# Loading two tiles of x from GpSimd's queue, dividing the fillers around their transposes, and storing one more late tile in halves

## The chip, the cores and the metric

The kernel runs on one core of a Trainium2 chip. The metric is the device time of one execution in microseconds. The kernel before has a median of 232.59 us over 3 runs.

## The reference

x is 16 x 512 x 1024 in bf16, that is 8192 tokens of 1024 values; w is 1024 x 1024 in bf16; b has 1024 values. In every column of w, each group of four successive rows keeps the two values of largest magnitude and sets the others to zero. The result is x times that pruned w, plus b.

```
wg = w.reshape(G, M, D)                     # M = 4
mag = jnp.abs(wg)
order = jnp.argsort(mag, 1)
thr = jnp.take_along_axis(mag, order[:, M - N:M - N + 1, :], 1)   # N = 2
mask = mag >= thr
wp = (wg * mask).reshape(D, D)
return jnp.einsum("bsd,df->bsf", x, wp) + b
```

## The kernel before, in words

The 8192 tokens are 64 tiles of 128. A tile's result is 128 x 1024: two PSUM banks of 512 columns, each the sum of eight matmuls over 128 values of the inner dimension.

TensorE cannot wait until all of w is pruned, so the work starts with seven tiles (0 to 6) that take the pruned w piece by piece. w is loaded in pieces (`load_w`, line 100); VectorE computes magnitude, threshold, mask and product of each (`Piece.do`, line 164; steps `abs`, `hi`, `lo`, `t1`, `t2`, `thr`, `mask`, `mult`). The first piece, columns 0 to 255 of the upper half of w, comes in two loads of 128 KB: one on SyncE's queue (lines 118 and 98), called w0a here, one on ScalarE's queue (line 119), called w0b. The seven tiles of x are loaded as they lie (`load_x`, line 103): tiles 5 and 6 on ScalarE's queue, tiles 3 and 4, tile 2, and tiles 0 and 1 on SyncE's. The loads are called x3, x5, x2 and x0 here, after their first tile. TensorE transposes them (`transpose`, line 188: four 128 x 128 transposes a tile, recorded at line 193; each needs the identity that GpSimd makes first), ScalarE copies the result to SBUF (`copy_xt`, line 196), and `mm_piece` (line 213) multiplies, recorded at line 229.

The order on each engine is written out by hand: `order` (line 266) lists tokens for TensorE, VectorE, ScalarE and SyncE, and the helper `seq` keeps each engine's instructions in that order. T3a is the transposes of tile 3, C3a its copy, M3.0yp a part of the multiplication of tile 3 with piece 0 (which follows the VectorE step mult0yp), W0.0 the spreading of pruned pieces into the natural layout `wp_nat` by DMA, E and A the first matmuls from that layout. A token F with a number is that many fillers; `order` has none before the change.

Ahead of the first transpose TensorE runs fillers (line 138): matmuls on constants whose result nobody reads. There are six of 512 columns and then fourteen of 128 columns (lines 404 and 405).

After the start, tiles 7 to 11 and the lower halves of tiles 0 to 6 use x that a DMA has transposed (`load_lead`, `load_low`), and tiles 12 to 63 come in batches by DMA transpose (`load_nat`). Each tile's result is evicted by VectorE with the bias (`evac`, line 435) and stored from ScalarE's queue (`store`, line 445). The last `LATE` tiles are stored in halves of 128 KB, the others whole, 256 KB.

Of the kernel before, what the change touches and what calls it, by code (L numbers as in the profile page):

```python
# [11 lines left out]
def kernel(  # L12
# [7 lines left out]
    nc = tc.nc  # L20
# [22 lines left out]
    STG = 8  # L43
    SOLO = 6
    GROUPS = ((0, 3), (3, 6), (6, 7))
    LATE = 6
    sizes = (4, 8, 8, 8, 8, 8, 8)
    batches = []
    t0 = NPK + LEAD
# [17 lines left out]
    def seq(eng, inst):  # L67
        if eng in tails:
            tc.add_manual_dep(inst.ins, tails[eng].ins.name, NOSYNC, reason="program order")
        tails[eng] = inst  # L70
        return inst

    def pe(i):
        return seq("pe", i)
# [4 lines left out]
    def act(i):  # L79
        return seq("act", i)  # L80
# [13 lines left out]
    bias_sb = const.tile([P, Dout], bf16)  # L94

    def issue(eng, out_, in_):
        q = nc.sync if eng == "sp" else nc.scalar
        return seq(eng, q.dma_start(out_, in_))

    def load_w(g, c0, c1, ma=0, mb=4, eng="sp"):  # L100
        issue(eng, w_sb[:, g, ma:mb, c0:c1], wv[:, g, ma:mb, c0:c1])

    def load_x(ta, tb, eng="sp"):
        xs = const.tile([P, tb - ta, HK], bf16, name=f"x_{ta}")
        issue(eng, xs[:], xf[ta * P:tb * P, :HK].rearrange("(t p) k -> p t k", p=P))
        for t in range(ta, tb):
            x_sb[t] = xs[:, t - ta, :]
# [7 lines left out]

    xnat, held = {}, {}

    load_w(0, 0, 256, 0, 2)
    load_w(0, 0, 256, 2, 4, "act")
    load_x(5, 7, "act")  # L120
    act(nc.scalar.activation(spark[:], nc.const_aps.tensor(1.0, [P, 1], bf16), Act.Abs))
    load_x(3, 5)
    load_x(2, 3)
    load_w(0, 256, 512)
    load_x(0, 2)
# [10 lines left out]
    def filler(n, rep=1):  # L136
        for _ in range(n):
            pe(nc.tensor.matmul(warm_ps[:, :rep * P], lhsT=nc.const_aps.tensor(1.0, [P, P], bf16),  # L138
                                rhs=nc.const_aps.tensor(1.0, [P, rep * P], bf16), start=True, stop=True))
# [4 lines left out]
    def spread(g, c0, c1, ks=range(4), eng="sp"):  # L144
        for k in ks:
            issue(eng, wp_nat[:, 4 * g + k, c0:c1], wp[32 * k:32 * k + 32, g, :, c0:c1])
# [112 lines left out]
    def stage(key):  # L259
        solo = key[1] == "h"  # L260
        q, h, at = (pair_of[key[0]], key[2], int(key[0] != SOLO)) if solo else (key[0], key[1] // 2, key[1] % 2)
        if (q, h) not in staged:
# [2 lines left out]

    order = {
# [124 lines left out]
    def run(queues):  # L391
        while any(queues.values()):
            moved = False
            for eng, toks in queues.items():
                while toks and all(n in written for n in needs(eng, toks[0])):
                    emit(eng, toks[0])
                    tok = toks.pop(0)
                    written.add(tok)
                    if tok[0] == "M" or tok[0].islower():
                        written.update(atoms(tok))  # L400
                    moved = True
            assert moved, queues

    filler(6, 4)
    filler(14)
    run({eng: order[eng].split() for eng in order})

    def load_nat(ta, tb):
# [26 lines left out]
    def evac(o, ps, c0, c1, add=None):  # L435
        if add is None:
            dve(nc.vector.tensor_tensor(o[:, c0:c1], ps, bias_sb[:, c0:c1], op=Alu.add))  # L437
        else:
            dve(nc.vector.tensor_tensor(o[:, c0:c1].rearrange("p (n c) -> p n c", n=2),  # L439
                                        ps.rearrange("p (n c) -> p n c", n=2), add, op=Alu.add))  # L440
# [4 lines left out]
    def store(eng, t, o, c0=0, c1=Dout):  # L445
        issue(eng, rows(t)[:, c0:c1], o[:, c0:c1])
# [25 lines left out]
    for bi, (tb, nb) in enumerate(batches):  # L472
        if bi:
            load_batch(bi + 1)
        for j in range(nb):
# [9 lines left out]
            else:  # L485
# [4 lines left out]
                for h in range(2):  # L490
                    evac(o, pss[h][:], h * FH, (h + 1) * FH)
                    if t >= NT - LATE:
                        store("act", t, o, h * FH, (h + 1) * FH)
                if t < NT - LATE:
                    store("act", t, o)
# [30 lines left out]
```

## Time and profile before

| what | value |
| --- | --- |
| median of 3 runs | 232.59 us (232.45 to 233.13) |
| the profiled execution's own time | 232.89 us |
| its span, first to last instruction | 231.1 us |
| TensorE matmul busy | 226.6 us, 98% of the span |
| VectorE busy | 107.9 us, 47% |
| ScalarE, GpSimd busy | 14.0 us, 17.6 us |

Times in the rows are microseconds from the start of the span. A row of the timeline gives the start, the time that the group took, the engine, the line, the operation, what it writes and reads, the shape and the count. PEld is TensorE's weight load. A row of a table by stage gives the stage's length, each engine's busy time with its count, the granted clock, the share of the DMA engines and the rate.

### The profile page before, as it was taken

How to read it: one execution, taken by the hardware profiler on the slowest of the kernel's cores; microseconds unless marked ns; L12 is line 12 of the kernel's file. 1: busy time of each engine (PE TensorE's matmuls, PEld its weight loads, DVE VectorE, ACT ScalarE, POOL GpSimd, SP SyncE). 2: the span in 40 equal slices, each digit the busy share in tenths (PEclk: the TensorE clock that was granted, in tenths of full speed). 3: DMA queues.
4: the chain of work that ended last, by engine and by line, in shares of the span. 5: the costliest groups of instructions: out<-in, count | busy, mean ns of one | idle time of the engine just before them, and what ended most of it. 6: DMA issues, size and time to landing. Idle time of an engine off the chain costs nothing.

```text
span 231.1 us, 2851 instructions
## 1 busy us (share of the span) xinstructions
PE 226.6 (98%) x1142; PEld 110.9 (48%) x1162; DVE 107.9 (47%) x200; ACT 14.0 (6%) x27; POOL 17.6 (8%) x15
## 2 busy tenths in 40 slices
PE   8999999999999999999999999999999999999995
PEld 5986444444444444444444444444444444444443
DVE  3999877844424424424424424423423423433434
ACT  2874100000000000000000000000000000000000
POOL 1000199700000000000000000000000000000000
PEclk9999999999999999999999999999999999999999
DMA  6999999997399422991259821693128932122122
GB/s 203 276 197 280 164 217 223 297 320 252 124 206 232 155 91 72 237 281 64 75 116 252 222 94 71 162 298 134 65 91 198 273 122 83 54 91 91 53 86 91
DMA packets 79308, 38.19 MB, mean 165 GB/s; under 512 B 64192, under 2 KB 71744, under 8 KB 79296
## 3 DMA queue, kind: packets, MB, share of 16 engines
q1 hardware_dynamic: 68384, 20.75, 43.6%
q10 hardware_dynamic: 10912, 17.27, 20.9%
q8 instruction: 9, 0.15, 0.3%
q14 instruction: 3, 0.02, 0.0%
HBM read 3.28 MB, written 16.78 MB: 87 GB/s over the span
## 4 chain that ended last, share of the span: by engine, by line
PE 98%; issue 0%; DVE 0%
PE ps L242 88%; PE ps L229 5%; PE tp L242 2%; PE ps L138 2%; PE tp L193 1%; PE ps L193 0%; DVE o L437 0%
## 5 line engine op out<-in xcount | busy, mean ns | idle before, releaser
L242 PE MATMUL ps<-wp_nat,xb 128*128 128x512 bf16 (+1 forms) x831 | 178.9, 375 | 0.9
L242 PEld LDWEIGHTS <-xb 128*128 128x128 bf16 x848 | 82.2, 98 | 97.7
L437 DVE TENSOR_TENSOR o<-ps,bias_sb 128x512 bf16<-128x512 f32 (+1 forms) x112 | 71.6, 677 | 113.7 <-PE ps L242 111.4
L433 POOL TENSOR_TENSOR st<-st,bias_sb 128x1024 f32<-128x1024 f32 x8 | 16.7, 2142 | 0.0
L242 PE MATMUL ps<-wp_nat,xlead 128*128 128x512 bf16 x63 | 14.7, 379 | 0.1
L242 PEld LDWEIGHTS <-xlead 128*128 128x128 bf16 x88 | 8.6, 98 | 10.2
L229 PE MATMUL ps<-wp,xt 128*128 128x256 bf16 (+1 forms) x130 | 12.8, 258 | 0.0
L439 DVE TENSOR_TENSOR o<-ps,st 128x512 bf16<-128x512 f32 x16 | 11.1, 691 | 2.8 <-PE ps L242 2.2
L229 PEld LDWEIGHTS <-xt 128*128 128x128 bf16 x130 | 10.9, 98 | 1.1
L242 PE MATMUL ps<-wp_nat,xlow 128*128 128x512 bf16 x47 | 10.6, 379 | 0.1
L264 ACT COPY st<-ps 128x512 f32<-128x512 f32 x14 | 7.4, 600 | 3.2 <-PE ps L229 3.1
L242 PEld LDWEIGHTS <-xlow 128*128 128x128 bf16 x48 | 4.7, 98 | 5.7
L159 DVE TENSOR_TENSOR mag<-mag,hi 128x256 bf16<-128x256 bf16 (+2 forms) x15 | 6.1, 435 | 0.1
L159 DVE TENSOR_TENSOR wp<-w_sb,mag 128x256 bf16<-128x256 bf16 (+2 forms) x15 | 6.1, 435 | 0.1
L242 PE MATMUL tp<-wp_nat,xlead 128*128 128x512 bf16 x23 | 5.8, 380 | 0.0
L138 PE MATMUL ps<-const-bfloat16-1.0 128*128 128x128 bf16 (+1 forms) x20 | 4.2, 408 | 0.8 <-PEq L510 0.8
L169 DVE TENSOR_SCALAR mag<-w_sb 128x512 uint16<-128x512 uint16 (+2 forms) x5 | 2.3, 473 | 3.5 <-DMA w_sb<-in_w_dram 3.5
L138 PEld LDWEIGHTS <-const-bfloat16-1.0 128*128 128x128 bf16 x20 | 2.3, 146 | 2.4 <-issue 2.4
L159 DVE TENSOR_TENSOR hi<-mag 128x512 bf16<-128x512 bf16 (+2 forms) x7 | 3.2, 458 | 0.1
L159 DVE TENSOR_TENSOR lo<-mag 128x512 bf16<-128x512 bf16 (+1 forms) x6 | 3.1, 509 | 0.0
L193 PEld LDWEIGHTS <-x 128*128 128x128 bf16 x28 | 2.3, 124 | 0.3 <-DMA x<-in_x_dram 0.2
L422 POOL COPY pruned<-wp 128x1 bf16<-128x1 bf16 x1 | 0.2, 187 | 26.7 <-DVE wp L159 26.7
(18 smaller groups left out, 18.8 us busy)
## 6 DMA issues: line engine op xcount, KB each, us to landing
out_dram<-o ACTq DMA_DIRECT2D x58, 256.0 KB, 2.4
wp_nat<-wp SPq DMA_DIRECT2D x14, 128.0 KB, 3.2
out_dram<-o ACTq DMA_DIRECT2D x10, 128.0 KB, 1.7
w_sb<-in_w_dram SPq DMA_DIRECT2D x2, 512.0 KB, 5.5
w_sb<-in_w_dram SPq DMA_DIRECT2D x3, 256.0 KB, 5.1
x<-in_x_dram SPq DMA_DIRECT2D x2, 256.0 KB, 4.3
x<-in_x_dram ACTq DMA_DIRECT2D x1, 256.0 KB, 4.0
bias_sb<-in_b_dram SPq DMA_DIRECT2D x1, 256.0 KB, 4.7
```

The lines of the kernel that those rows point to most:

```text
L138: pe(nc.tensor.matmul(warm_ps[:, :rep * P], lhsT=nc.const_aps.tensor(1.0, [P, P], bf16), rhs=nc.const_aps.tensor(1.0, [P, rep * P], bf16), ...
L159: dve(nc.vector.tensor_tensor(out, a, b_, op=op))
L169: dve(nc.vector.tensor_single_scalar(mag.bitcast(u16), w_.bitcast(u16), 0x7FFF, op=Alu.bitwise_and))
L193: pe(nc.tensor.transpose(tp[:, m, :], xg[:, m, :], ident[:]))
L229: pe(nc.tensor.matmul(ps[:, c0 + d:c1 + d], lhsT=xpk[t][:, m, :], rhs=wp[:, g, m, c0:c1], start=(new and m == ms.start), stop=(left[key] = ...
L242: pe(nc.tensor.matmul(ps, lhsT=xt[:, kt - koff, :], rhs=wp_nat[:, kt, c0:c1], start=(kt == first), stop=(kt == last)))
L264: act(nc.scalar.copy(staged[(q, h)][:, at, :, :].rearrange("p t c -> p (t c)"), ps_open.pop(key)[:]))
L422: pool(nc.gpsimd.tensor_copy(out=pruned[:], in_=wp[:, 1, 3, Dout - 1:]))
L433: pool(nc.gpsimd.tensor_tensor(st[:], st[:], bias.to_broadcast([P, 2, 2, CW]), op=Alu.add))
L437: dve(nc.vector.tensor_tensor(o[:, c0:c1], ps, bias_sb[:, c0:c1], op=Alu.add))
L439: dve(nc.vector.tensor_tensor(o[:, c0:c1].rearrange("p (n c) -> p n c", n=2), ps.rearrange("p (n c) -> p n c", n=2), add, op=Alu.add))
```

## The change

Tiles 3 and 4 of x are no longer loaded from SyncE's queue, in its second place, but from GpSimd's, ahead of the identity. Of the fourteen narrow fillers four stay ahead of the transposes of tiles 3 and 4; six more stand behind these, ahead of the transposes of tiles 5 and 6; four are gone. `LATE` goes from 6 to 7, so tile 57 is stored in two halves.

```diff
-    LATE = 6
+    LATE = 7
...
     def issue(eng, out_, in_):
-        q = nc.sync if eng == "sp" else nc.scalar
+        q = {"sp": nc.sync, "act": nc.scalar, "pool": nc.gpsimd}[eng]
         return seq(eng, q.dma_start(out_, in_))
...
+    load_x(3, 5, "pool")
     load_w(0, 0, 256, 0, 2)
     load_w(0, 0, 256, 2, 4, "act")
     load_x(5, 7, "act")
     act(nc.scalar.activation(spark[:], nc.const_aps.tensor(1.0, [P, 1], bf16), Act.Abs))
-    load_x(3, 5)
     load_x(2, 3)
...
-            "T3a T4a T5a T6a T2a M3.0yp M4.0yp M3.0yq M4.0yq M5.0y M6.0y M3.0u M4.0u M3.0v M4.0v M6.0u M6.0v M5.0u "
+            "T3a T4a F6 T5a T6a T2a M3.0yp M4.0yp M3.0yq M4.0yq M5.0y M6.0y M3.0u M4.0u M3.0v M4.0v M6.0u M6.0v M5.0u "
...
     filler(6, 4)
-    filler(14)
+    filler(4)
```

In the program that results, the first transpose waits for the load of GpSimd's queue and for the identity, which GpSimd makes behind it. SyncE's queue holds one load less at its start, and the semaphores of the hardware queues are handed out one place earlier from there to the store of tile 57.

## The prediction

> **What bounds the kernel now.** I read the page first, its shares and its chain.
>
> ```profile
> span 231.1 us, 2851 instructions
> PE 226.6 (98%) x1142; PEld 110.9 (48%) x1162; DVE 107.9 (47%) x200; ACT 14.0 (6%) x27; POOL 17.6 (8%) x15
> PE 98%; issue 0%; DVE 0%
> PE ps L242 88%; PE ps L229 5%; PE tp L242 2%; PE ps L138 2%; PE tp L193 1%; PE ps L193 0%; DVE o L437 0%
> ```
>
> TensorE is the chain, from the fillers of line 138 to the last matmul, so the end moves only if TensorE begins its useful work at another time, works at another rate, or comes to wait. All edits but one lie in the first seven microseconds, so I read the timeline of that stage next.
>
> ```profile
> 0.73 0.45 SPq L98 DMA_DIRECT2D w_sb<-in_w_dram  x1
> 0.74 0.50 ACTq L98 DMA_DIRECT2D w_sb<-in_w_dram  x1
> 0.77 4.21 PE L138 MATMUL ps<-const-bfloat16-1.0 128*128 128x512 bf16 x20 [0.77 <-PEq L510]
> 1.01 0.29 POOL masks.py:199 TENSOR_SCALAR_AFFINE_SELECT ident<-ident 128x128 bf16<-128x128 bf16 x1
> 1.24 0.96 SPq L98 DMA_DIRECT2D x<-in_x_dram  x2
> 1.26 0.49 ACTq L98 DMA_DIRECT2D x<-in_x_dram  x1
> 3.50 0.49 DVE L169 TENSOR_SCALAR mag<-w_sb 128x512 uint16<-128x512 uint16 x2 [3.50 <-DMA w_sb<-in_w_dram]
> 4.96 1.62 PEld L193 LDWEIGHTS <-x 128*128 128x128 bf16 x20 [0.24 <-DMA x<-in_x_dram]
> 5.80 0.48 DVE L159 TENSOR_TENSOR wp<-w_sb,mag 128x256 bf16<-128x256 bf16 x2
> 5.80 0.72 PE L193 MATMUL ps<-ident,x 128*128 128x128 bf16 x8
> 6.35 0.39 PE L193 MATMUL tp<-ident,x 128*128 128x128 bf16 x4
> 6.58 1.92 PE L229 MATMUL ps<-wp,xt 128*128 128x128 bf16 x20
> ```
>
> The fillers end shortly before x3 lands; the transposes run from 4.96 to 6.58 without a gap; then the first piece is multiplied. From 4.96 on TensorE is never without work, so what the change can give is decided by when the multiplications, now at 6.58, begin. Two more chains meet there. VectorE started at 3.50, when w0a was there, and its first product ends at 5.80 plus one operation:
>
> ```profile
> L159 DVE TENSOR_TENSOR wp<-w_sb,mag x4: 279/280/283, 5.8 to 6.8; 128x256 bf16<-128x256 bf16 x4
> ```
>
> That is 6.08, so VectorE is 0.50 us ahead of TensorE. This is the cap: however early the transposes are, with VectorE as it is the multiplications begin no sooner than 6.08. The second chain is TensorE's own rate, which the granted clock (1.00 in every stage) does not show but the weight loads do:
>
> ```profile
> 0.77:3.28 2.51, 2.51 (x6) 0.86 (x7) 1.00 0.42 122
> 3.28:4.78 1.50, 1.50 (x15) 1.43 (x13) 1.00 1.07 375
> 4.96:6.01 1.05, 1.05 (x10) 1.05 (x11) 1.00 1.04 307
> 6.01:6.58 0.57, 0.57 (x12) 0.57 (x10) 1.00 1.09 334
> ```
>
> Six wide fillers take 2.51 us; the fourteen narrow ones 1.50 us, 0.107 us each; the transposes take 1.05/11 = 0.095 to 0.105 us until 6.01, and 0.57/10 = 0.057 us after. So TensorE's rate doubles at 6.01, 5.24 us after its first matmul at 0.77. The rows above of fillers are those of line 138, the others those of line 193.
>
> **The change part by part.** *The fillers.* The first four narrow ones end at 3.28 + 4 x 0.107 = 3.71, where TensorE now wants tiles 3 and 4. The six behind T4 cost 0.64 us at the slow rate and 0.34 us at the fast one, unless TensorE would wait for x5 anyway.
>
> *x3 on GpSimd's queue.* No load of that queue is in the trace, so I bound its landing by the loads that are.
>
> ```profile
> w_sb<-in_w_dram SPq DMA_DIRECT2D x1, 128.0 KB, 2.7
> x<-in_x_dram SPq DMA_DIRECT2D x1, 256.0 KB, 3.7
> x<-in_x_dram ACTq DMA_DIRECT2D x1, 256.0 KB, 4.0
> w_sb<-in_w_dram ACTq DMA_DIRECT2D x1, 128.0 KB, 2.9
> x<-in_x_dram SPq DMA_DIRECT2D x1, 128.0 KB, 4.0
> x<-in_x_dram SPq DMA_DIRECT2D x1, 256.0 KB, 5.0
> 1.75:2.50 0.75, 0.75 (x4) 0.22 (x2) 0.00 (x0) 0.71 (x1) 0.00 (x0) 1.00 0.45 118
> 2.50:3.25 0.75, 0.75 (x3) 0.23 (x2) 0.00 (x0) 0.74 (x2) 0.00 (x0) 1.00 0.93 276
> 3.25:4.00 0.75, 0.75 (x8) 0.71 (x7) 0.50 (x3) 0.04 (x1) 0.00 (x0) 1.00 1.04 368
> 4.00:4.75 0.75, 0.75 (x10) 0.72 (x7) 0.75 (x4) 0.00 (x0) 0.00 (x0) 1.00 1.09 380
> ```
>
> These are issues in the first six microseconds, with the time from issue to landing, and the rate in the last column. GpSimd can issue at 0.73. With the shortest time here, 2.7 us, x3 would land at 3.43; with the longest of a load of its size, 5.0 us, at 5.73. Between them the bytes decide. The stages moved 88, 207, 276 and 285 kB. w0a, w0b and x3 are 524 kB, reached at 3.25 + (524 - 295)/368 = 3.87. Between the bytes and the landing there is a tail: w0a and w0b together, 262 kB, were through at 3.13, and w0b landed at 0.74 + 2.9 = 3.64, 0.5 us later. So if the DMA engines did nothing else, x3 would land at about 4.4; it landed at 1.24 + 3.7 = 4.94 with x5 beside it. Since x2 and x5 still share, I take 4.6. The engines are full from 2.50 on (0.93 and more), so an earlier issue cannot make all loads early: it changes whose bytes come first.
>
> The Trainium skill gives a price of its own, "DMA: Bandwidth & Descriptors", section "Anatomy of one DMA": about 2.0 us plus the bytes over 436 GB/s for a load of this queue, and by that 262 kB would land 2.6 us after the issue, at 3.33, ahead of the fillers' end at 3.71. No load of this kernel has that queue yet; the loads of 256 KB on the other two took 3.7 to 5.0 us.
>
> *What x3 takes from w0b.* w0b, issued at 0.74 and landed at 3.64, is under way just when x3 would be. Its landing now lies between 3.64, undisturbed, and 4.4, with all three through together; I take 4.0. The second `abs` on VectorE, now at 3.7, waits for it, and behind it the whole pruning, so VectorE's first product moves from 6.08 to about 6.4. The slack of 0.50 us hides that; 0.75 us it would not.
>
> *x5 and x2.* x5 landed at 1.26 + 4.0 = 5.3, x2, issued half a microsecond after x3, at about 1.7 + 4.0 = 5.7. As all five loads are the same bytes as before, I leave them there, within 0.5 us; T5 will not ask sooner than 5.3.
>
> *The sum.* T3 and T4 run from 4.6 for 8 x 0.105 = 0.84 us, to 5.44. Of the six fillers 5.3 fit before 6.01, the rest takes 0.04: 6.05. T5 and T6 take 8 x 0.057 = 0.46: 6.51. T2 takes 0.23: 6.74. The multiplications begin at 6.74 instead of 6.58, with VectorE ready at 6.4. That is a loss of 0.16 us, and 232.89 becomes 233.05 us. The median of the runs is 0.30 us under the profiled execution; such a run would be held by VectorE's 0.3 us instead, which again takes most of the difference. I forecast 233.0 us, no change by the bound of 0.3% (0.7 us), which is about what a measurement of this kernel can tell.
>
> *Edits at nothing.* The identity was ready at 1.30 and is wanted no sooner than 3.71, so GpSimd may spend 2.4 us on the issue (the same load took SyncE half of 0.96 us); if it spends more, the identity binds T3 in x3's place. SyncE's later issues come up to 0.5 us sooner, but the loads on its queue land behind the same bytes. The change of `LATE` adds one issue on ScalarE's queue, at tile 57.
>
> ```profile
> 222.03 7.10 ACTq L98 DMA_DIRECT2D out_dram<-o  x6
> out_dram<-o ACTq DMA_DIRECT2D x58, 256.0 KB, 2.4
> out_dram<-o ACTq DMA_DIRECT2D x10, 128.0 KB, 1.7
> ```
>
> Six such issues sit in the last 7.10 us and none holds TensorE; one more is hidden: it lands in 1.7 us, six tiles of 16 matmuls of 512 columns before the end, or 6 x 16 x 4 x 0.057 = 22 us, and it sets the semaphores of the last stores back in their old places.
>
> **The rivals.** *The rate doubles later (slower).* Between 3.71 and x3's landing TensorE now stands idle, by my sum 0.9 us, where before it stood idle 0.24 us at most. If the doubling needs as long a run without a break as before, it comes at 4.6 + 5.24 = 9.84. Then T3 to T2 with the fillers end at 4.6 + 0.84 + 0.64 + 0.84 + 0.42 = 7.34, and the 2.50 us from there to 9.84 do 1.25 us of multiplications; before, that point was reached at 6.58 + 1.25 = 7.83. The loss is 2.0 us: 234.9 us. It decides from the point where the idle time is long enough, somewhere between 0.24 us, which did no harm, and all of the 0.9. For it: nothing else explains a doubling at 6.01 than TensorE's own activity. Against: the trace has no longer gap that shows the threshold. The Trainium skill, "TensorE: Matmul & The Clock Gate", Part 1, has the rate rise after a busy window of about 3.4 us that runs freely, and Part 4 says that transposes don't count in the same way. By that rule the window that ends at 6.01 would hold 1.7 us of fillers after the change instead of 2.2, and a miss would put the doubling at 9.4 and the time at about 234.7 us. Chance 0.34.
>
> *x3 lands late (slower, less so).* If GpSimd's queue gets a third of the rate beside x5 and x2, x3 lands at 5.7. T3 and T4 then end at 6.30, the fillers at 6.64, T5, T6 and T2 at 7.33: a loss of 0.75 us, 233.6 us. For it: in the trace x3 was ahead of x2 in one queue, and no longer is. Against: GpSimd issues 0.5 us sooner than SyncE did. Chance 0.16, a quarter of it within the bound.
>
> *x3 lands by 3.7 (gain).* Then T3, T4 and the fillers end at 3.71 + 0.84 + 0.64 = 5.19, T5 begins at 5.3 and T2 ends at 6.28; if w0b is hardly late, the multiplications gain 0.3 us: 232.6 us, or 232.3 on the median's footing. Against: 524 kB can't be through by 3.2. The cap of 0.50 us keeps even this within the bound but for a small part. Chance 0.12, of which 0.04 faster.
>
> That the edit does nothing, because the loads land where they did, is within the forecast.
>
> **How the numbers follow.** The forecast has 0.38, and its own range is 232.4 to 233.4 (x3 at 4.2 to 4.9, w0b at 3.64 to 4.4). Within 0.3%: 0.38 + 0.04 + 0.08 = 0.50. Slower: 0.34 + 0.12 = 0.46. Faster: 0.04. The range runs from the gain's 232.3 to the late doubling's 234.9.
>
> **What would show it.** Right: the first weight load of line 193 stands at about 4.6 with an idle time of some 0.9 us put down to x3's DMA, VectorE's second `abs` near 4.0, line 229 first at about 6.7, and the weight loads' spacing halves near 6.0. Late doubling: the spacing stays at 0.1 us beyond 9. Late x3: the first transpose beyond 5.5. Wrong altogether: x3 there before 3.71 and line 229 before 6.4, or a TensorE wait behind 7 us, at T0 or the first matmuls from `wp_nat`, which had none.

## The result and the profile after

The change makes the kernel slower: 235.66 us (median of 4 runs, 235.17 to 236.76) against 232.52 us (median of 4, 232.44 to 233.13), a ratio of 1.0139 with a 95% interval of 1.0117 to 1.016. The profiled execution took 235.17 us, the shortest of its four; that of before took 232.89 us.

The first lines of the page after, its row for the new queue and its chain:

```profile
span 233.4 us, 2846 instructions
PE 227.0 (97%) x1138; PEld 111.4 (48%) x1158; DVE 107.9 (46%) x200; ACT 14.3 (6%) x27; POOL 18.4 (8%) x16
q0 software_dynamic: 80, 0.26, 0.3%
PE 96%; DMA 2%; issue 1%; DVE 0%; POOLq 0%
```

A load now stands in the chain with 2% of the span. The timeline of the start shows which, and what follows from it:

```profile
1.24 0.84 POOL L98 DMA_DIRECT2D x<-in_x_dram  x1 [0.79 <-POOLq L510]
2.38 0.29 POOL masks.py:199 TENSOR_SCALAR_AFFINE_SELECT ident<-ident 128x128 bf16<-128x128 bf16 x1
3.30 0.36 PEld L138 LDWEIGHTS <-const-bfloat16-1.0 128*128 128x128 bf16 x3 [0.28 <-issue]
3.51 0.49 DVE L169 TENSOR_SCALAR mag<-w_sb 128x512 uint16<-128x512 uint16 x2 [3.51 <-DMA w_sb<-in_w_dram]
5.78 0.78 PEld L193 LDWEIGHTS <-x 128*128 128x128 bf16 x8 [2.12 <-DMA x<-in_x_dram]
5.81 0.48 DVE L159 TENSOR_TENSOR wp<-w_sb,mag 128x256 bf16<-128x256 bf16 x2
6.52 0.68 PEld L138 LDWEIGHTS <-const-bfloat16-1.0 128*128 128x128 bf16 x6
7.16 1.32 PEld L193 LDWEIGHTS <-x 128*128 128x128 bf16 x12
8.44 2.01 PEld L229 LDWEIGHTS <-xt 128*128 128x128 bf16 x20
```

GpSimd begins its issue at 1.24, half a microsecond behind the first issues of the other queues, and is at it for 0.84 us. TensorE's weight loads stop behind the fillers and wait 2.12 us for x3; T3 begins at 5.78 instead of 4.96. All twenty transposes and the six fillers then run at the slow rate: 8 in 0.78 us, 6 in 0.68, 12 in 1.32, about 0.107 us each. The first loads of the multiplications, 1.69 us for 20 before, take 2.01 us. VectorE is where it was: 3.51 and 5.81 instead of 3.50 and 5.80.

The table of weight loads by stage (length, busy time and count, granted clock, DMA share, rate) shows that the rate is still the slow one up to 9.08:

```profile
5.78:7.16 1.38, 1.38 (x15) 1.00 1.09 324
7.16:8.44 1.28, 1.28 (x14) 1.00 1.18 302
8.44:9.08 0.64, 0.64 (x8) 1.00 1.10 325
```

The six loads that begin in the third stage are still 0.107 us apart; the counts take in loads that reach over the borders. The seventh, at 9.08, is the last of them, and behind it they are 0.056 us apart; before, that came at 6.01. Where both kernels are past it, the same step of the chain can be compared, before and after:

```profile
9.16 10.30 PE ps L229 x108
```
```profile
1.24 4.50 DMA x<-in_x_dram
11.39 10.30 PE ps L229 x108
```

The 108 multiplications take 10.30 us in both and begin 2.23 us later. The spans differ by 2.3 us, so everything happens ahead of this step. Of the 2.23 us, 1.9 lie in the later start of the multiplications (8.44 and 6.52 by their weight loads) and 0.3 in their first stretch, still slow. The medians differ by 3.1 us. Only the profiled executions have traces, so the reason is argued: the moment of the doubling is not the same in every execution (the traces below have it between 3.5 and 11.6), and after the change it costs more when it is late.

### The profile page after: what moved, and what is told of

It reads as the page before. It is cut to its first block, busy times and chain, and to the rows that moved or that the text cites. A ratio compares the mean times of both kernels' runs of the same rounds, so it can differ in the third digit from the quotient of the medians.

```text
span 233.4 us, 2846 instructions
## 1 busy us (share of the span) xinstructions
PE 227.0 (97%) x1138; PEld 111.4 (48%) x1158; DVE 107.9 (46%) x200; ACT 14.3 (6%) x27; POOL 18.4 (8%) x16
## 3 DMA queue, kind: packets, MB, share of 16 engines
HBM read 3.28 MB, written 16.78 MB: 86 GB/s over the span
## 4 chain that ended last, share of the span: by engine, by line
PE 96%; DMA 2%; issue 1%; DVE 0%; POOLq 0%
PE ps L242 87%; PE ps L229 5%; PE tp L242 2%; DMA x<-in_x_dram 2%; PE tp L193 1%; PE ps L193 0%; PE ps L138 0%; DVE o L437 0%; POOLq L510 0%; POOLq masks.py:199 0%
## 5 line engine op out<-in xcount | busy, mean ns | idle before, releaser
L193 PE MATMUL tp<-ident,x 128*128 128x128 bf16 x16 | 2.1, 287 | 1.9 <-DMA x<-in_x_dram 1.9
L193 PEld LDWEIGHTS <-x 128*128 128x128 bf16 x28 | 2.8, 136 | 2.1 <-DMA x<-in_x_dram 2.1
```

The costliest lines, as they stand in the source:

```text
L193: pe(nc.tensor.transpose(tp[:, m, :], xg[:, m, :], ident[:]))
```

## The experiments

Medians are in us, each beside the kernel before on the same chip.

**Keeping TensorE busy until x3 is there.** In the kernel after:

```diff
-            "T3a T4a F6 T5a ...
+            "T3a T4a T5a ...
...
-    filler(4)
+    filler(23)
```

> The kernel after, with 23 narrow fillers ahead of the first transpose instead of 4 and none behind tile 4: TensorE has work until x3 lands at 5.74. Theory (the idle time of 2 us before x3 lands puts off the doubling of TensorE's rate): the doubling comes back to about 6, the multiplications begin near 7.0, and only the late landing is left: 232.9 to 233.2 us. Rival (the late landing and the slow rate have nothing to do with the idle time; the doubling stays near 9): T3 at 5.78, 20 transposes at 0.107 us, then slow to 9: about 235.0 us.

233.36 us against 232.57, ratio 1.0031 (1.0018 to 1.0044).

```profile
3.29 2.39 PEld L138 LDWEIGHTS <-const-bfloat16-1.0 128*128 128x128 bf16 x22 [0.28 <-issue]
5.88 1.15 PEld L193 LDWEIGHTS <-x 128*128 128x128 bf16 x20 [0.20 <-DMA x<-in_x_dram]
6.98 1.69 PEld L229 LDWEIGHTS <-xt 128*128 128x128 bf16 x20
```

x3 is as late as in the change, but the twenty transposes take 1.15 us instead of 2.1: the rate has doubled by 5.9. So it is the idle time that puts the doubling off, as the theory had it. Without it 0.8 us of the 3.1 are left, a little more than expected; T3 begins 0.92 us later than in the kernel before, and that is the late landing.

**The fillers of the change alone**, in the kernel before:

```diff
-            "T3a T4a T5a ...
+            "T3a T4a F6 T5a ...
...
-    filler(14)
+    filler(4)
```

> The kernel before with the fillers of the change alone: 4 narrow ones ahead of the first transpose, 6 behind tile 4; x3 stays on SyncE's queue and lands at 4.92, so TensorE idles 1.1 us. Theory (idle time puts the doubling off): it comes near 9.4 in place of 6.0, and 234.2 to 234.7 us. Rival (only a longer idle time does, or only x3's landing counts): the doubling stays near 6, the six fillers cost 0.3 us: 232.8 to 233.0 us.

234.52 us (234.36 to 234.78), ratio 1.008 (1.0065 to 1.0095).

```profile
4.98 0.78 PEld L193 LDWEIGHTS <-x 128*128 128x128 bf16 x8 [1.33 <-DMA x<-in_x_dram]
5.71 0.68 PEld L138 LDWEIGHTS <-const-bfloat16-1.0 128*128 128x128 bf16 x6
6.35 1.32 PEld L193 LDWEIGHTS <-x 128*128 128x128 bf16 x12
7.63 2.13 PEld L229 LDWEIGHTS <-xt 128*128 128x128 bf16 x20
```

x3 lands on time, and yet the loss is 2.0 us: after 1.33 us without a weight load everything stays slow beyond 7.63, and the spacing halves only near 8.5. The division of the fillers does harm by itself.

**The load alone on GpSimd's queue**: the kernel before with `load_x(3, 5, "pool")` ahead of the other loads, fourteen fillers, none behind T4.

> The kernel before with the load alone moved to GpSimd's queue: 14 narrow fillers, none behind tile 4, so TensorE idles from 4.78 to x3's landing at 5.74, about 1 us. Theory (idle time puts the doubling off): near 9, the multiplications begin near 7.9: 234.3 to 234.7 us. Rival (1 us does no harm, it takes the 2 us of the change): the doubling stays near 6, only the late landing is left, 233.0 us.

233.74 us, ratio 1.0065 (1.0037 to 1.0093). The seven runs fall into two groups: 233.28 to 233.93 (five) and 235.22 and 235.32 (two). The profiled execution is of the first:

```profile
3.29 1.21 PEld L138 LDWEIGHTS <-const-bfloat16-1.0 128*128 128x128 bf16 x13 [0.28 <-issue]
5.86 1.15 PEld L193 LDWEIGHTS <-x 128*128 128x128 bf16 x20 [1.36 <-DMA x<-in_x_dram]
6.95 1.69 PEld L229 LDWEIGHTS <-xt 128*128 128x128 bf16 x20
```

Thirteen loads of the fillers take 1.21 us here, where they took 1.43 in the kernel before: their spacing falls from 0.107 to 0.06 us near 4.2, ahead of the idle time. The 1.36 us without a weight load that follow did not undo the doubling, but this trace cannot show whether they would have put it off. Two runs of seven lost what the theory expected. They may be those in which the rate had not doubled when the fillers ended; no trace of them shows it.

**A shorter idle time**: the kernel before with 10 narrow fillers in place of 14.

> The kernel before with 10 narrow fillers in place of 14: the idle time ahead of T3 grows from 0.2 to about 0.6 us and nothing else changes. If the rate doubles only after a window of 3.4 us that is nearly full, most runs miss one: 233.5 to 234.5 us. If a window that is 82% full does, no change: 232.5 us.

232.72 us against 232.56, ratio 1.0007 (0.9995 to 1.0019), and none of the ten runs is above 233.19.

```profile
3.29 0.65 PEld L138 LDWEIGHTS <-const-bfloat16-1.0 128*128 128x128 bf16 x9 [0.28 <-issue]
5.05 1.15 PEld L193 LDWEIGHTS <-x 128*128 128x128 bf16 x20 [1.12 <-DMA x<-in_x_dram]
```

At the slow rate the fillers would end at 3.28 + 10 x 0.107 = 4.35 and leave about 0.6 us, an estimate, and no run shows harm from that. But the profiled execution is not such a case: its spacing falls near 3.5, among the fillers, and the 1.12 us without a weight load come behind the doubling and did not undo it. So four fillers and 1.33 us lost 2 us in every run, and 0.6 us probably loses nothing; where between them it turns is open.

**Transposes in the place of fillers**, in the kernel before:

```diff
-    filler(14)
+    fill_tp = warm_ps[:].bitcast(bf16)[:, :P]
+    for _ in range(14):
+        pe(nc.tensor.transpose(fill_tp, ident[:], ident[:]))
```

> The kernel before with its 14 narrow fillers turned into as many transposes of the identity, at the same places and of the same size; nothing else changes. If transposes count as activity for the rate as matmuls do: the doubling stays near 6, 232.5 us as before. If they do not: the doubling comes a window later, near 9.4, T3 to T2 take 2.1 us, and about 234.2 us.

232.56 us against 232.57, ratio 1.0002 (0.9993 to 1.0012).

```profile
3.29 1.43 PEld L407 LDWEIGHTS <-ident 128*128 128x128 bf16 x13 [0.28 <-issue]
4.73 1.95 PEld L193 LDWEIGHTS <-x 128*128 128x128 bf16 x20
```

The spacing halves near 6.4, behind 3.1 us of nothing but transposes. They bring the doubling as matmuls do. The Trainium skill, "TensorE: Matmul & The Clock Gate", Part 4, says that transposes don't count as busy in the same way; this measurement disagrees, and it decides.

**The change without its six fillers behind T4.**

> The kernel after without the six fillers behind tile 4. Theory (at the slow rate they only push work back 0.64 us, and about half of that is got back because the doubling does not move): 0.3 us less than the change, about 235.3 us. Rival (they keep TensorE active and hold the doubling early): slower than the change.

235.09 us, ratio 1.0108 (1.0076 to 1.0139), against 235.66 and 1.0139 (1.0117 to 1.016) for the change, which ran in another set. By the medians the six fillers cost 0.5 to 0.6 us, but the intervals overlap. Nothing here speaks for the rival, that they held the rate up. The profiled execution, 236.05 us and the slowest of the four, shows how far the doubling can be put off: the twenty first loads of the multiplications take 3.25 us, and the spacing halves only near 11.6.

```profile
5.79 2.06 PEld L193 LDWEIGHTS <-x 128*128 128x128 bf16 x20 [2.13 <-DMA x<-in_x_dram]
7.80 3.25 PEld L229 LDWEIGHTS <-xt 128*128 128x128 bf16 x20
```

**One more tile in halves**: the kernel before with `LATE = 7`.

> The kernel before with tile 57 stored in halves (LATE 7) and nothing else. Theory (hidden, one more issue 22 us before the end): 232.5 us, no change. Rival (the stores of the last tiles pass to other semaphores and wait): slower by 0.2 us or more.

232.61 us against 232.44, ratio 1.0002 (0.9989 to 1.0015): no change that these runs can tell.

```profile
4.66 1.19 PEld L193 LDWEIGHTS <-x 128*128 128x128 bf16 x20
```

The start of this kernel is that of the kernel before, and yet its rate doubles near 4.6 and not at 6.01: the moment varies by itself.

**Another load on GpSimd's queue**: tiles 0 and 1 instead of 3 and 4, in the kernel before.

> The kernel before with the load of tiles 0 and 1, wanted at 8.2 us, moved to GpSimd's queue in place of that of tiles 3 and 4. If only the moment at which x3 is wanted makes GpSimd's queue dear, this load lands near 5.7, ahead of its use: 232.5 us, no change. If a load of that queue harms as such (it delays the others, or the identity), T3 begins later than 4.96 and the time is 232.9 us or more.

233.80 us against 232.44, ratio 1.0053 (1.0036 to 1.0071). The expectation of no change was wrong, and the sign that it gave for harm, a T3 later than 4.96, was wrong as well: T3 began early, at 4.66. The weight loads, tile 2's load and the table by stage (its last column is the rate):

```profile
4.66 0.93 PEld L193 LDWEIGHTS <-x 128*128 128x128 bf16 x16 [0.30 <-DMA x<-in_x_dram]
6.82 0.26 PEld L193 LDWEIGHTS <-x 128*128 128x128 bf16 x4 [1.24 <-DMA x<-in_x_dram]
```
```profile
x<-in_x_dram SPq DMA_DIRECT2D x1, 128.0 KB, 5.0
```
```profile
4.75:5.50 0.75, 0.75 (x15) 0.75 (x16) 0.75 (x7) 0.39 (x2) 0.00 (x0) 1.00 0.82 240
5.50:6.25 0.75, 0.24 (x5) 0.09 (x2) 0.75 (x6) 0.75 (x3) 0.00 (x0) 1.00 0.61 193
```

T2 waits 1.24 us for tile 2, which is still on SyncE's queue and lands 5.0 us after its issue instead of 4.0. In these two stages the rate is 240 and 193 GB/s, where the kernel before had 299 and 335. That GpSimd's load lowers the rate is not shown: in the change its packets moved mostly from 4.00 to 5.50, where all queues together had 350 and 322 GB/s. Why tile 2 is late here stays open.

**What makes x3 late.** Two kernels from the one with 23 fillers. In the first, x5 stands behind ScalarE's table load and activation.

> The kernel with x3 on GpSimd's queue and 23 fillers, but the load of tiles 5 and 6 is issued behind ScalarE's table load, at 3.3 in place of 1.27. If x3 lands late because x5 and the others share the engines with it, it now lands near 5.0. If GpSimd's queue itself starts late (first packet near 3.9), x3 lands hardly sooner, at 5.4 to 5.7. The time is not the point: tiles 5 and 6 are late here.

This one tells nothing on the question: the profile has x5's issue at 1.33 all the same, beside the table load, and T3 at 6.10. In the second, x5 and x2 wait until GpSimd has written a column of their tiles, and so are issued at 2.23 and 2.26.

> The kernel with x3 on GpSimd's queue and 23 fillers, where the loads x5 and x2 (and SyncE's loads behind x2) are held back until GpSimd has written one column of their tiles behind its issue of x3, so that from about 3.3 to 3.8 us nothing but x3 asks for the DMA engines. If x3 waited for the engines in the change, its first packets now come near 3.0 to 3.3 and it lands by 4.8. If GpSimd's queue starts late of itself, the first packet stays near 3.9 and x3 lands at 5.2 to 5.7. The time is not the point: x5 and x2 are late here.

The rows of the DMA view for the time from 0 to 3.25 us, among them the issue's time to landing, and the stage behind it:

```profile
q0 software_dynamic: 9, 0.04, 13.2%
...
x<-in_x_dram POOLq DMA_DIRECT2D x1, 256.0 KB, 4.4
```
```profile
3.25:4.00 0.75, 0.75 (x8) 0.71 (x7) 0.43 (x3) 0.74 (x2) 0.00 (x0) 1.00 0.60 118
```

In the kernel after, no packet of that queue, q0, came before 3.75; with the others held back, nine came before 3.25. To that extent it had waited. But then, with almost nothing beside it until 4.00, it moved at most 118 GB/s, and x3 landed 4.4 us after its issue, at 5.64, as against 4.5 in the change. The expectation of 4.8 for a load that only waits for the engines did not come true. So in this one trace sharing is not what makes x3 late; from 4.00 on other loads were beside it again. What holds the load back the runs don't show: in the change the same queue moved 0.17 MB from 4.00 to 4.75, faster than here.

**Two versions meant to beat both**: the kernel before with x3 and x5 loaded tile by tile, and one with x3 alone loaded so and tile 2 on ScalarE's queue, both with ten narrow fillers.

> A version meant to beat both: the kernel before with x3 and x5 each loaded in two parts of one tile (128 KB) on the same queues, and 10 narrow fillers, so that T3 can begin when tile 3 alone has landed, near 4.4. If the transposes gain 0.4 us, the multiplications begin up to 0.4 us sooner in the runs where VectorE does not hold them: 232.2 to 232.4 us. If the further issues (0.5 us each) push tiles 2 and 6 back, 232.6 us or more.

232.99 us against 232.56, ratio 1.002 (1.0009 to 1.0031).

> A second version meant to beat both: the kernel before with x3 in two parts of one tile on SyncE's queue, and to keep the number of SyncE's issues, tile 2 on ScalarE's queue behind x5; 10 narrow fillers. If the transposes begin near 4.3 and x0 lands by 8.0 as before, the multiplications begin up to 0.4 us sooner in the runs where the rate doubles late: 232.2 to 232.5 us. If the parts land later than the whole did, or x0 does, 232.8 us or more.

232.96 us against 232.53, ratio 1.0017 (0.9997 to 1.0038). Eleven of its runs lie between 232.79 and 233.30, one at 234.94. Neither beats the kernel before. T3 begins at 4.24 and 4.17, but something else lands later: in the first, whose profiled execution is the slowest of its twelve, tile 0 (T0 at 8.83 behind 1.05 us of waiting), in the second, tile 4 (1.21 us behind T3).

```profile
8.83 0.26 PEld L195 LDWEIGHTS <-x 128*128 128x128 bf16 x4 [1.05 <-DMA x<-in_x_dram]
```
```profile
5.64 0.93 PEld L194 LDWEIGHTS <-x 128*128 128x128 bf16 x16 [1.21 <-DMA x<-in_x_dram]
```

## Why the prediction was wrong

The forecast was 233.0 us with no change; 235.66 lies outside its range.

**The sum left the doubling at 6.01.** It made TensorE idle 0.9 us ahead of T3 and still let T5, T6 and T2 run at the fast rate. In the profile TensorE idled 2.1 us and the rate doubled at 9.1. This is the larger part of the loss, about 1.9 of the 3.1 us: with no filler behind T4 and x3 late, four fillers lost 2.65 us (235.09 against 232.44) and 23 lost 0.79 (233.36 against 232.57).

**The landing of x3 was mis-sized**: 4.6 was taken and 5.74 measured (1.24 + 4.5). The far bound, 5.73, met it by luck, as 0.73 + 5.0. Two things failed. The issue was put at 0.73 and began at 1.24. And the bytes were taken to decide: no packet of the load came before 3.75, and with GpSimd's load almost alone on the engines for a time, x3 landed hardly earlier, at 5.64. The estimate by the Trainium skill's price, "DMA: Bandwidth & Descriptors", section "Anatomy of one DMA", is 2.6 us for such a load, far from the 4.4 and 4.5 us measured here, even counted from the issue's start.

**The two slower rivals were kept apart, and they came together.** Late landing was priced at 0.75 us; measured without the idle time it is 0.8. The late doubling was priced at 2.0 us; the fillers alone, with x3 on time, cost 2.0. Each price came out, the second although the doubling stood near 8.5 in that trace and not at 9.84. But the later x3 lands, the longer TensorE idles, so the first brings the second. The sum had no case for it, and the range ended at 234.9. That the two prices, 2.75 us, lead from 232.89 to the measured 235.6 is in part luck: from the median, 232.52, they lead to 235.3, and the profiled execution lost 2.3 us.

**The six fillers** were charged 0.04 us, because the doubling was to come in their midst. It came behind them. By the medians they cost 0.5 to 0.6, which is not clear of the noise.

**What held.** That TensorE's own activity brings the doubling, and idle time ahead of it puts it off, is shown by two pairs: four fillers ahead of T3 against fourteen with x3 on time, and four against 23 with x3 late. The threshold was left between 0.24 and 0.9 us; the runs leave it open up to 1.33, with 0.6 probably harmless. The identity, ready at 2.67, and the further half stores were hidden, as said. VectorE was expected 0.3 us late by w0b and was not late at all, since x3's packets came behind w0b's; the cap that VectorE sets never came into play in the change.

The rule of the Trainium skill, "TensorE: Matmul & The Clock Gate", Part 1, a window of about 3.4 us that runs freely, agrees with what the runs show: kernels with the same start have their doubling at different moments (6.01 and near 4.6). That the window runs freely no run shows by itself.

## What to carry to other kernels

Fillers ahead of the first real work have to last until that work's data is there: an idle time of 1.33 us ahead of the doubling cost 2 us here, more than the late data itself (0.8), while up to 1.36 us of idle time behind the doubling did not bring the slow rate back. When two slow cases have the same cause, work out the time of both together and give it a chance of its own. A queue is chosen by the measured time from issue to landing, and not by the free slot on its engine: the load moved to spare SyncE half a microsecond landed 0.8 us later.

## What the runs showed of the hardware

- A load of 256 KB from GpSimd's queue landed 4.4 to 4.8 us after its issue in the six traces with tiles 3 and 4 on it, and 5.2 us in the one with tiles 0 and 1; the issue itself took 0.84 us and began at 1.24, where the other queues began at 0.74.
- With almost nothing beside it, from 3.25 to 4.00, it moved at most 118 GB/s; in the change, beside others, 0.17 MB from 4.00 to 4.75.
- The spacing of TensorE's weight loads halved at moments from about 3.5 (ten fillers) to about 6.4 us (transposes as fillers) where TensorE idled no more than 0.24 us ahead of that, and near 8.5, 9.1 and 11.6 where TensorE idled 1.33 to 2.13 us ahead of it. The granted clock read 1.00 in these stages.
- Once the spacing had halved, 1.12 to 1.36 us without a weight load did not undo it (three traces: ten fillers, tiles 0 and 1 on GpSimd's queue, the load alone).
- Transposes bring the doubling as matmuls do (232.56 and 232.57 us; 3.1 us of transposes ahead of it).
- A DMA issue that stands behind ScalarE's activation and its table load in the order did not wait for them: it began at 1.33, the table load at 1.27, the activation at 2.56.
